# Float64 weights split into two float32r parts: from sums on the tensor engine to a 16-bit addition and subtractions on the vector engine, with a new order of the first steps

## The chip, the cores and the metric

The kernel runs on one core of one Trainium2 chip. The metric is the device time of one execution in microseconds (us); several executions are timed and the median is given.

## The reference

The kernel computes a chunked attention and then a feed-forward layer with a softmax-linear-unit. q, k and v have the shape (8, 8, 576, 64): batch, heads, sequence, head dimension. The attention is local to chunks of 64 positions. The weights `w_in` (512 x 1024) and `w_out` (1024 x 512) arrive as float64; the rest is float32.

```
scores = scale * q_c @ k_c.T          # per chunk of 64, scale = 1/sqrt(64)
attn   = exp(scores - max) / (sum + 1e-9)
x      = (attn @ v_c) as (4608 tokens, 512)
h      = x @ w_in                     # 4608 x 1024
solu   = h * softmax(h)
ln     = (solu - mean) / sqrt(var + 1e-6) * g_ln
out    = ln @ w_out                   # 4608 x 512, float32
```

## The kernel before, in words

The 4608 tokens are 36 tiles of 128. For each tile i the steps are: q and k with the head dimension on the partitions, scores (`scores`), softmax (`softmax_a`, `softmax_e`, `softmax_b`), the transposed attention, the products with v (`values`), the split of x into a high and a low float32r part (`x_high`, `x_low`), the first layer (`ffn_in`, 24 matmuls of 128x512 into the PSUM tile `ph`, which has one buffer), the maximum of h and the exponential (`solu_a`), the product and the mean (`solu_b`), the variance (`variance`), the transposed z and its split, and the second layer (`ffn_out`, 24 matmuls into a PSUM tile `po`, in three thirds of eight). Each float32 product is three float32r products: high by low, high by high and low by high.

The first five tiles and the preparation of the weights are written out by hand in the string `START` (from line 19). A word there is one step; a step that yields is named again for each further part, so `N:0:0` stands twice, first for the transposes on the tensor engine and then for the copy out of PSUM. The order of the words is the order of the instructions in every engine's queue (tensor PE, vector DVE, scalar ACT, GpSimd POOL, and SP, which issues most DMAs); a program behind the kernel places the semaphores, and each engine works its queue strictly in order. From tile 5 on (`for i in range(first, NT)`) a regular loop takes over. Its first large step is `ffn_in(5)`, called M:5 below.

The words that matter here: `P` loads a unit of raw weights (units 0 to 3 are 128 rows each of `w_in`, units 4 to 7 are 256 rows each of `w_out`, 1 MB each; `P0` and `P1` load unit 0 in halves), `n` loads q and k of a tile naturally, `v` loads v, `g` loads the gains, `q` loads q and k in transposable blocks for later tiles. `N` transposes q or k of a tile on PE, `S` is the scores, `A` and `B` the softmax, `T` the transposes of the attention, `V` the values and the split of x, `M` the first layer, `X` and `Y` the two halves of the solu, `R` the variance, `Z` and `z` the turn of z, `F` a third of the second layer and `o` its store.

A unit of weights is prepared like this before the change. Of each float64 the upper 32-bit word, read as a float32, is clamped (`c`, first part: POOL, for unit 4 DVE, 128x1024), rescaled by an activation (`c`, second part: ACT) and shifted left by three bits on DVE (`C`): that is the float64 cut off to float32, the tile `w_a`. ACT rounds it to float32r, times the gain for `w_out` (`t`, the tiles `wi_h`, `wo_h`). DVE masks the exponent (`r`, into `w_p`) and multiplies it with the lower word (into `w_r`): the rest that the cut lost. The low part is then a sum in PSUM (`D`, `unit_rest`, twice a unit): the identity times `w_a`, minus the high part, plus `w_r`; three matmuls written, four executed, because the float32 one runs as two. For `w_out` the identity is a diagonal of gains that POOL makes. The sum in `po` is then copied to `wi_l` or `wo_l`, by ACT, or by DVE for the two pairs in `EV_DVE`.

PSUM before: `ph` two banks, `sx` two banks (scores and values of a tile in START), `tp` two banks (the transposes of START through `bank()`; in the loop the same banks are the second `sx`, named `sy`), `po` two buffers of one bank (sums of `unit_rest` and of the second layer). The tail uses `bank()` as well: the two transposes of the last tile's z, and one half of the last output.

Of the kernel before, what the change touches and what calls it, by code (L numbers as in the profile page):

```python
# [57 lines left out]
def chunk_attention_then_solu_ffn(  # L58
# [10 lines left out]
    nc = tc.nc  # L69

    B, H, S, D = q.shape
    DM, FF = H * D, g_ln.shape[0]
    P = 128
# [10 lines left out]

    EV_DVE = ((1, 0), (5, 1),)
    NV_DVE = ((0, 0), (0, 1), (1, 0), (1, 1), (3, 0), (6, 0), (9, 1),)
# [22 lines left out]

    TP = ps_t.tile([P, 2, FF // 2], F32, name="tp")  # L110
    banks = 0

    def bank():
        nonlocal banks
        banks += 1
        return TP[:, banks % 2]

# [6 lines left out]
    g_sb = const.tile([P, NFC], F32, name="g_sb")  # L124
    ident_r = const.tile([P, P], F32R, name="ident_r")
    nc.vector.tensor_copy(out=ident_r, in_=ident)
    minus_r = const.tile([P, P], F32R, name="minus_r")
    nc.vector.tensor_scalar(
        out=minus_r, in0=ident, scalar1=-1.0, scalar2=None, op0=ALU.mult
    )  # L130


    const.tile([P, 80], F32, name="pad")
    wi_h = const.tile([P, NCC, FF], F32R, name="wi_h")
# [33 lines left out]

    scaled, tops, lows, diags = {}, {}, {}, {}

    def unit_scale(x):

        hi = raws[x][:, :, :, 1]
        y = scaled[x] = work.tile([P, 2, HALF], F32, name="w_a")
# [7 lines left out]
    def unit_top(x):  # L186
# [13 lines left out]
        tops[x] = a, lo  # L200

    def unit_high(x):
        kind, m = UNITS[x]
        a, lo = tops[x]
# [8 lines left out]
        tops[x] = a, lo, top  # L213

    def unit_low(x):
        kind, m = UNITS[x]
        a, lo = tops[x][:2]
        au = a.bitcast(U32)
        r = work.tile([P, 2, HALF], F32R, name="w_r")
        ru = work.tile([P, 2, HALF], U32, name="w_p2", tag="a_b", bufs=1)  # L220
        dve.tensor_scalar(
            out=ru, in0=au, scalar1=0xFF800000, scalar2=None, op0=ALU.bitwise_and
        )
        dve.scalar_tensor_tensor(
            out=r, in0=lo, scalar=2.0 ** -52, in1=ru.bitcast(F32),
            op0=ALU.mult, op1=ALU.mult,
        )
        if kind == "out":
            for y in range(2):
                one = small.tile([P, P], F32, name="g_diag", bufs=2)  # L230
                one_r = small.tile([P, P], F32R, name="g_diag_r", bufs=2)
                for t in (one, one_r):
                    pool.tensor_scalar(
                        out=t, in0=ident, scalar1=g_sb[:, 2 * m + y:2 * m + y + 1],
                        scalar2=0.0, op0=ALU.mult, op1=ALU.add,
                    )
                diags[x, y] = one, one_r
        lows[x] = r

    def unit_rest(x, y):  # L240

        kind, m = UNITS[x]
        (a, _, top), r = tops[x], lows[x]
        if kind == "in":
            one, one_r = ident, ident_r
            d = wi_l[:, m, y * HALF:(y + 1) * HALF]
        else:
            one, one_r = diags.pop((x, y))
            d = wo_l[:, 2 * m + y, :]
# [101 lines left out]

    st = {}


    sx = ps_a.tile([P, 2, 2, HP, CH], F32, name="sx")
    sy = TP.rearrange("p j (s a k) -> p j s a k", s=2, k=CH)

    def attn(i):
        return sy if order.on and i % 2 else sx

    def scores(i):
        sx = attn(i)
        for hp in range(HP):
            for c in range(2):
                for j in range(2):
                    rows, cols = slice(j * D, (j + 1) * D), slice(c * CH, (c + 1) * CH)
                    pe.matmul(
                        sx[cols, j, 0, hp],
                        QT[i][rows, hp, cols],
                        KT[i][rows, hp, cols],  # L370
                        start=True,
                        stop=True,
                    )
# [6 lines left out]
    def softmax_a(i):  # L380
        sv = attn(i)[:, :, 0].rearrange("p j a k -> p a j k")
        nmax = small.tile([P, HP, 2], F32, name="s_nmax")
# [76 lines left out]
    def values(i):  # L459
        sx = attn(i)  # L460
        for hp in range(HP):
            for j in range(2):
                for c in range(2):
                    rows = slice(c * CH, (c + 1) * CH)
                    pe.matmul(
                        sx[j * D:(j + 1) * D, c, 1, hp],
                        V[i][rows, 2 * hp + j, :],
# [17 lines left out]
    def x_high(i):  # L485
        xv = attn(i)[:, :, 1].rearrange("p c a t -> p a c t")
        xh = work.tile([P, NCC, P], F32R, name="x_h")
# [5 lines left out]
    def x_low(i):  # L493
        xv = attn(i)[:, :, 1].rearrange("p c a t -> p a c t")
        xhv, xlv = (x.rearrange("p a (c t) -> p a c t", t=CH) for x in st[i, "x"])
        dve.tensor_tensor(out=xlv, in0=xv, in1=xhv.bitcast(F32), op=ALU.subtract)
# [33 lines left out]
    def solu_b(i):  # L530
# [15 lines left out]
        st[i, "z"] = z, esum  # L546

    def variance(i):
# [17 lines left out]
    def z_turn(i):  # L566
        z, _ = st[i, "n"]
        if i % 2 == 0:
# [30 lines left out]
    def z_transpose(i, f):  # L599

        z, _ = st[i, "n"]
        pt = bank().rearrange("p (a t) -> p a t", t=P)
# [125 lines left out]
    def product():  # L728
# [8 lines left out]
        "T": attn_transpose, "U": attn_turn, "V": start_values, "c": unit_scale,  # L737
        "C": unit_top, "t": unit_high, "r": unit_low, "D": unit_rest, "M": ffn_in, "X": solu_a, "Y": solu_b,
        "R": variance, "Z": z_turn, "z": z_half, "F": product, "o": store,
# [124 lines left out]
```

## Time and profile before

| | |
|---|---|
| median of three timed executions | 502.07 us (503.82, 501.36, 502.07) |
| span of the profiled execution | 501.8 us; no other time of that execution is listed |
| instructions | 11184 |
| tile 5's first layer (M:5) begins | 106.62 us |
| granted TensorE clock, mean over the span | 0.997 |

Times in the views are us from the span's start. A row of the windows gives a stretch, its length, the busy time of PE, PE's weight loads, DVE, ACT and POOL with counts in brackets, the granted clock of PE, the share of the DMA engines and GB/s. A row of the grouped instructions gives line, engine, operation, output<-inputs, shapes and count, then the total busy us, the mean ns of one, and the idle time before them with what ended it. All instructions of the ordered engines carry one line (L49, a helper), so the groups are told apart by tile names. A matmul's modelled duration is longer than the time between two of them, because they overlap: 24 matmuls of 128x512 with 0.39 us each take about 5.45 us in a row.

### The profile page before, as it was taken

What the parts mean: (1) busy time and instruction counts of PE and PEld (TensorE: products, weight loads), DVE (VectorE), ACT (ScalarE), POOL (GpSimd) and SP (SyncE); (2) the same over time, 40 slices, a digit from 0 to 9 for tenths busy, and PEclk for the clock granted to TensorE, in tenths of its full rate; (3) what the DMA queues carried; (4) which work ended last, traced back from release to release, by engine and by line L of the source; (5) the groups of instructions that cost most, each with busy time, mean ns of one, the idle gap of its engine ahead of it and who ended that gap; (6) DMA issues with size and microseconds to landing.
All of it is one profiled execution on the core that took longest, in us unless ns stands there. A gap on an engine that the chain in (4) does not pass through costs nothing.

```text
span 501.8 us, 11184 instructions
## 1 busy us (share of the span) xinstructions
PE 482.5 (96%) x4248; PEld 391.5 (78%) x4248; DVE 376.7 (75%) x529; ACT 261.7 (52%) x434; POOL 146.4 (29%) x305
## 2 busy tenths in 40 slices
PE   2799998999999999999999999999999999999997
PEld 1467676788888888888888888888888888888876
DVE  3697886659795988787878787878887887954430
ACT  2578875445454555545464545545455454544451
POOL 2124340153241325050505051505142323323300
PEclk9999998999999999999999999999999999999999
DMA  9986884594968687869725778767771716153211
GB/s 267 317 180 169 175 151 103 100 216 82 208 121 185 126 182 170 176 158 163 173 58 146 148 176 142 182 112 194 125 189 35 193 34 183 45 145 85 65 62 42
DMA packets 195908, 72.57 MB, mean 145 GB/s; under 512 B 180048, under 2 KB 180560, under 8 KB 195472
## 3 DMA queue, kind: packets, MB, share of 16 engines
q1 hardware_dynamic: 189008, 58.49, 53.6%
q0 software_dynamic: 6272, 12.60, 9.7%
q10 hardware_dynamic: 576, 0.79, 0.5%
q8 instruction: 33, 0.54, 0.5%
q14 instruction: 19, 0.16, 0.1%
HBM read 37.23 MB, written 9.44 MB: 93 GB/s over the span
## 4 chain that ended last, share of the span: by engine, by line
PE 92%; ACT 4%; DVE 1%; issue 1%; DMA 1%; ACTq 0%; SPq 0%
PE po L49 42%; PE ph L49 39%; PE tp L49 7%; PE sx L49 5%; ACT attn_t L49 1%; DMA nat<-in_q_dram 1%; ACT wo_h L49 1%; ACT z L49 0%; ACT z_h L49 0%; ACT o_sb L49 0%; DVE s_e L49 0%; DVE qT L49 0%; DVE h_nmax L49 0%; ACT kT L49 0%; ACT qT L49 0%
## 5 line engine op out<-in xcount | busy, mean ns | idle before, releaser
L49 PE MATMUL ph<-wi_l,x_h 128*128 128x512 f32 x288 | 113.5, 394 | 0.0
L49 PE MATMUL ph<-wi_h,x_h 128*128 128x512 f32 x288 | 112.8, 392 | 0.0
L49 PE MATMUL po<-wo_l,z_h 128*128 128x512 f32 x280 | 111.2, 397 | 0.1
L49 PE MATMUL po<-wo_h,z_l 128*128 128x512 f32 x280 | 109.5, 391 | 0.0
L49 PE MATMUL po<-wo_h,z_h 128*128 128x512 f32 x280 | 109.3, 391 | 0.0
L49 ACT ACTIVATE z<-ph,h_nmax 128x1024 f32<-128x1024 f32 x36 | 40.2, 1116 | 132.1 <-DVE h_nmax L49 132.0
L49 POOL TENSOR_TENSOR u<-ssq,eps 128x1 f32<-128x1 f32 x36 | 7.2, 200 | 247.9 <-ACT sq L49 247.9
L49 PE MATMUL ph<-wi_h,x_l 128*128 128x512 f32 x288 | 78.0, 389 | 0.0
L49 POOL DMA_DIRECT2D z_t<-z_b x136 | 67.7, 505 | 17.0 <-DVE z_b L49 15.2
L49 DVE TENSOR_REDUCE h_nmax<-ph 128x1 f32<-128x1024 f32 x36 | 44.0, 1223 | 36.7 <-PE ph L49 36.7
L49 PEld LDWEIGHTS ph<-wi_l,x_h 128*128 128x128 f32 x288 | 54.6, 190 | 11.7 <-PE po L49 0.4
L49 PEld LDWEIGHTS ph<-wi_h,x_h 128*128 128x128 f32 x288 | 54.6, 190 | 11.3
L49 PEld LDWEIGHTS ph<-wi_h,x_l 128*128 128x128 f32 x288 | 54.1, 188 | 11.4
L49 PEld LDWEIGHTS po<-wo_l,z_h 128*128 128x128 f32 x280 | 52.5, 188 | 11.9 <-ACT z_h L49 0.5
L49 PEld LDWEIGHTS po<-wo_h,z_l 128*128 128x128 f32 x280 | 52.6, 188 | 11.6 <-DVE z_l L49 0.6
L49 PEld LDWEIGHTS po<-wo_h,z_h 128*128 128x128 f32 x280 | 52.6, 188 | 10.5
L49 DVE TENSOR_TENSOR z_l<-z_t,z_h 128x1024 fp32r<-128x1024 f32 (+1 forms) x35 | 40.7, 1163 | 20.4 <-ACT z_h L49 20.4
L49 DVE SCALAR_TENSOR_TENSOR z<-ph,z 128x1024 f32<-128x1024 f32 x36 | 43.9, 1220 | 14.9 <-ACT z L49 14.9
L49 ACT ACTIVATE z<-z,z_sum 128x1024 f32<-128x1024 f32 x32 | 36.9, 1154 | 22.2 <-DVE z L49 21.6
L49 DVE STREAM_TRANSPOSE z_b<-z 128x1024 f32<-128x1024 f32 x33 | 40.0, 1211 | 6.2 <-ACT z L49 3.1
L49 ACT ACTIVATE o_sb<-po,r 128x512 f32<-128x512 f32 (+1 forms) x36 | 24.2, 673 | 31.5 <-POOL r L49 20.3
L49 ACT ACTIVATE sq<-z 128x1024 bf16<-128x1024 f32 x36 | 37.5, 1043 | 0.1
(99 smaller groups left out, 656.4 us busy)
## 6 DMA issues: line engine op xcount, KB each, us to landing
out_dram<-o_sb SPq DMA_DIRECT2D x33, 256.0 KB, 2.5
v_sb<-in_v_dram SPq DMA_DIRECT2D x32, 256.0 KB, 4.3
z_t<-z_b POOLq DMA_DIRECT2D x128, 64.0 KB, 2.7
z_t<-z_b SPq DMA_DIRECT2D x128, 64.0 KB, 2.9
q_st<-in_q_dram SPq DMA_DIRECT2D x96, 72.0 KB, 3.2
k_st<-in_k_dram SPq DMA_DIRECT2D x96, 72.0 KB, 3.1
w_raw<-in_moe_w_out_dram SPq DMA_DIRECT2D x4, 1024.0 KB, 7.4
attn_t<-a_b POOLq DMA_DIRECT2D x60, 64.0 KB, 3.6
```

The costliest lines, as they stand in the source:

```text
L49: ins = make(*args, **kwargs)
```

## The change

- `unit_low` (`r`) and the sums of `unit_rest` on PE are gone, with `ident_r`, `minus_r`, the tiles `w_r`, `w_p`, and the diagonals on POOL.
- `C` becomes `unit_round`: after the shift, a second DVE instruction adds the lower word, times 2^-29, to the lower 16 bits of each float32, as unsigned 16-bit numbers with a step of two. It turns the cut into a rounding to float32, and what is below float32 is dropped.
- `D` becomes a subtraction on DVE, 128x512, in one part: the rounded weight (times the gain for `w_out`) minus its high part. All its operands lie in SBUF.
- `bank()` returns a buffer of `po` in place of half of `tp`, so the transposes of START and of the tail share two buffers with the sums of the second layer. `sy` has its two banks alone; in START the scores of a tile go to `sx` and its values to `sy`.
- `w_a` has four buffers instead of two.
- `START` is written anew. The same words stand in it, apart from `r` (gone), `C` (two parts) and `D` (one part), in another order: q and k of tiles 0 and 1 are loaded ahead of the weights, units 3 and 7 earlier, and the blocks `q` later. The loop from tile 5 is the same.

```diff
 START (before)
-P0 n:0 v:0 P1 P:1 n:1 P:2 v:1 P:3 N:0:0 N:0:1 N:0:0 n:2 N:0:1 g P:4 S:0 c:0 A:0 c:0 A:0 C:0 B:0
-c:1 t:0 c:1 r:0 T:0 T:0 N:1:0 C:1 N:1:1 D:0:1 N:1:0 t:1 r:1 D:0:0 D:0:1 V:0 N:1:1 D:0:0 c:2
-D:1:1 V:0 v:4 n:3 c:2 V:0 D:1:0 D:1:1 C:2 M:0 r:2 t:2 c:3 S:1 D:1:0 c:3 D:2:0 A:1 N:2:0 D:2:0
-N:2:1 C:3 D:2:1 N:2:0 n:4 r:3 N:2:1 P:5 t:3 M:0 v:3 P:6 A:1 c:4 D:3:1 D:2:1 B:1 c:4 D:3:0 D:3:1
-M:0 D:3:0 C:4 r:4 t:4 T:1 M:0 T:1 N:3:1 X:0 V:1 N:3:1 D:4:0 X:0 S:2 D:4:0 Y:0 N:3:0 V:1 N:4:1
...
 START (after)
+n:0 N:0:0 N:0:1 n:1 N:0:0 N:1:0 N:0:1 S:0 N:1:1 P0 N:1:0 P1 A:0 N:1:1 c:0 P:3 P:1 A:0 n:2 P:2
+v:0 c:0 B:0 c:3 C:0 c:1 n:3 S:1 N:2:1 C:0 c:3 t:0 A:1 D:0:0 N:2:0 c:1 C:3 A:1 c:2 N:2:1 C:1 C:3
+T:0 P:7 N:2:0 C:1 n:4 S:2 P:4 N:3:0 B:1 T:0 c:2 t:3 N:3:1 A:2 C:2 A:2 N:3:0 C:2 t:1 v:1 N:3:1
+V:0 P:6 v:2 D:0:1 n:5 S:3 g P:5 V:0 T:1 D:1:1 V:0 T:1 A:3 M:0 N:4:0 N:4:1 c:7 D:1:0 N:4:0 t:2
+B:2 v:5 n:6 D:3:1 A:3 c:4 D:2:0 D:2:1 M:0 T:2 D:3:0 B:3 T:2 V:1 v:7 c:6 M:0 c:5 N:4:1 M:0 c:4
+X:0 N:5:0 V:1 c:6 S:4 V:1 X:0 N:5:0 N:5:1 C:6 V:2 V:2 Y:0 c:7 C:4 v:3 N:5:1 C:6 V:2 T:3 M:1 c:5
+C:4 T:3 N:6:1 N:6:0 A:4 n:7 N:6:1 C:5 X:1 S:5 Y:0 z:0:1 v:4 X:1 t:6 C:7 V:3 N:6:0 z:0:0 Y:1 M:2
+z:0:1 n:8 z:0:0 t:4 V:3 C:5 C:7 z:0:1 z:0:0 A:5 t:5 N:7:0 R:0 A:4 N:7:0 Q:2 N:7:1 D:4:0 S:6 q:8
+D:5:0 N:7:1 N:8:1 N:8:0 D:4:1 X:2 N:8:1 q:8 X:2 B:4 Y:2 V:3 A:6 N:8:0 D:6:0 n:9 Y:1 A:5 F t:7
+Y:2 T:4 D:5:1 T:4 Z:2 B:5 M:3 X:3 R:2 V:4 A:6 S:7 D:7:1 T:5 D:6:1 D:7:0 F F B:6 X:3 T:5 V:4 q:8
+o:0 V:4 Y:3 q:8 Y:3 v:6 z:1:1 V:5 z:1:0 z:1:0 z:1:1 M:4 A:7 Z:3 U:6 z:1:0 R:3 N:9:0 A:7 z:1:1
+N:9:0 F X:4 B:7 R:1 N:9:1 F X:4 U:7 N:9:1 F Y:4 V:5 o:1 Y:4 V:5 R:4

 bank
-        nonlocal banks
-        banks += 1
-        return TP[:, banks % 2]
+        return ps_o.tile([P, FF // 2], F32, name="po")
...
 unit_round (was unit_top), after the shift by three
+        yield
+        half = a.bitcast(U16).rearrange("p x (n two) -> p x n two", two=2)[:, :, :, 0]
+        dve.scalar_tensor_tensor(
+            out=half, in0=lo, scalar=2.0 ** -29, in1=half, op0=ALU.mult, op1=ALU.add
+        )
...
 unit_low: removed
-        dve.tensor_scalar(
-            out=ru, in0=au, scalar1=0xFF800000, scalar2=None, op0=ALU.bitwise_and
-        )
-        dve.scalar_tensor_tensor(
-            out=r, in0=lo, scalar=2.0 ** -52, in1=ru.bitcast(F32),
-            op0=ALU.mult, op1=ALU.mult,
-        )
...
 unit_rest
-        ps = ps_o.tile([P, HALF], F32, name="po")
-        pe.matmul(ps, one, a[:, y], start=True, stop=False)
-        pe.matmul(ps, minus_r, top[:, y], start=False, stop=False)
-        pe.matmul(ps, one_r, r[:, y], start=False, stop=True)
-        yield
-        if (x, y) in EV_DVE:
-            dve.tensor_copy(out=d, in_=ps)
-        else:
-            act.copy(d, ps)
+            dve.tensor_tensor(
+                out=wi_l[:, m, y * HALF:(y + 1) * HALF], in0=a[:, y],
+                in1=top[:, y].bitcast(F32), op=ALU.subtract,
+            )
+        else:
+            dve.scalar_tensor_tensor(
+                out=wo_l[:, 2 * m + y, :], in0=a[:, y],
+                scalar=g_sb[:, 2 * m + y:2 * m + y + 1],
+                in1=top[:, y].bitcast(F32), op0=ALU.mult, op1=ALU.subtract,
+            )
...
 attention tiles
-    sy = TP.rearrange("p j (s a k) -> p j s a k", s=2, k=CH)
+    sy = ps_t.tile([P, 2, 2, HP, CH], F32, name="sy")
-    def attn(i):
-        return sy if order.on and i % 2 else sx
+    def attn(i, part):
+        return (sx, sy)[i % 2 if order.on else part][:, :, part]
```

More of the change, by code (lines that the diff above doesn't have):

```diff
@@ L11 @@
 U32 = mybir.dt.uint32
+U16 = mybir.dt.uint16
 AF = mybir.ActivationFunctionType
@@ L82, in chunk_attention_then_solu_ffn @@
     assert FF == 32 * 32
-    EV_DVE = ((1, 0), (5, 1),)
     NV_DVE = ((0, 0), (0, 1), (1, 0), (1, 1), (3, 0), (6, 0), (9, 1),)
@@ L106, in chunk_attention_then_solu_ffn @@
     )
-    TP = ps_t.tile([P, 2, FF // 2], F32, name="tp")
-    banks = 0
     def bank():
-        nonlocal banks
-        banks += 1
-        return TP[:, banks % 2]
+        return ps_o.tile([P, FF // 2], F32, name="po")
     ident = const.tile([P, P], F32, name="ident")
@@ L124, in chunk_attention_then_solu_ffn @@
     g_sb = const.tile([P, NFC], F32, name="g_sb")
[L125 to L129, printed above, removed]
-    )
-    const.tile([P, 80], F32, name="pad")
+    const.tile([P, 336], F32, name="pad")
     wi_h = const.tile([P, NCC, FF], F32R, name="wi_h")
@@ L167, in load_pair @@
         raws[x] = raw
-    scaled, tops, lows, diags = {}, {}, {}, {}
+    scaled, tops = {}, {}
     def unit_scale(x):
         hi = raws[x][:, :, :, 1]
-        y = scaled[x] = work.tile([P, 2, HALF], F32, name="w_a")
+        y = scaled[x] = work.tile([P, 2, HALF], F32, name="w_a", bufs=4)
         top = 1.875 * 2.0 ** 16
@@ L184, in unit_scale, with unit_round @@
         act.activation(y, y, AF.Prelu, scale=2.0 ** -112, alpha=-(2.0 ** 32))
-    def unit_top(x):
+    def unit_round(x):
         kind, m = UNITS[x]
@@ L199, in unit_top @@
         )
-        tops[x] = a, lo
+        yield
[3 more added lines that the diff above has]
+        )
+        tops[x] = a
     def unit_high(x):
         kind, m = UNITS[x]
-        a, lo = tops[x]
+        a = tops[x]
         if kind == "in":
@@ L212, in unit_high @@
                 act.activation(top[:, y], a[:, y], AF.Copy, scale=g)
[L213 to L220, printed above, removed]
-        dve.tensor_scalar(
-            out=ru, in0=au, scalar1=0xFF800000, scalar2=None, op0=ALU.bitwise_and
-        )
-        dve.scalar_tensor_tensor(
-            out=r, in0=lo, scalar=2.0 ** -52, in1=ru.bitcast(F32),
-            op0=ALU.mult, op1=ALU.mult,
[L227 to L238, printed above, removed]
+        tops[x] = a, top
     def unit_rest(x, y):
         kind, m = UNITS[x]
-        (a, _, top), r = tops[x], lows[x]
+        a, top = tops[x]
         if kind == "in":
-            one, one_r = ident, ident_r
-            d = wi_l[:, m, y * HALF:(y + 1) * HALF]
-        else:
-            one, one_r = diags.pop((x, y))
-            d = wo_l[:, 2 * m + y, :]
-        ps = ps_o.tile([P, HALF], F32, name="po")
-        pe.matmul(ps, one, a[:, y], start=True, stop=False)
-        pe.matmul(ps, minus_r, top[:, y], start=False, stop=False)
-        pe.matmul(ps, one_r, r[:, y], start=False, stop=True)
-        yield
-        if (x, y) in EV_DVE:
-            dve.tensor_copy(out=d, in_=ps)
-        else:
-            act.copy(d, ps)
+            dve.tensor_tensor(
+                out=wi_l[:, m, y * HALF:(y + 1) * HALF], in0=a[:, y],
+                in1=top[:, y].bitcast(F32), op=ALU.subtract,
+            )
+        else:
+            dve.scalar_tensor_tensor(
[3 more added lines that the diff above has]
+            )
     QT, KT, V, QS, KS = {}, {}, {}, {}, {}
@@ L349, in turn_natural @@
             act.copy((QT, KT)[x][i], pt)
-    st = {}
+    st, ZS = {}, {}
     sx = ps_a.tile([P, 2, 2, HP, CH], F32, name="sx")
-    sy = TP.rearrange("p j (s a k) -> p j s a k", s=2, k=CH)
-    def attn(i):
-        return sy if order.on and i % 2 else sx
+    sy = ps_t.tile([P, 2, 2, HP, CH], F32, name="sy")
+    def attn(i, part):
+        return (sx, sy)[i % 2 if order.on else part][:, :, part]
     def scores(i):
-        sx = attn(i)
+        s = attn(i, 0)
         for hp in range(HP):
@@ L367, in scores @@
                     pe.matmul(
-                        sx[cols, j, 0, hp],
+                        s[cols, j, hp],
                         QT[i][rows, hp, cols],
@@ L380, in softmax_a @@
     def softmax_a(i):
-        sv = attn(i)[:, :, 0].rearrange("p j a k -> p a j k")
+        sv = attn(i, 0).rearrange("p j a k -> p a j k")
         nmax = small.tile([P, HP, 2], F32, name="s_nmax")
@@ L459, in values @@
     def values(i):
-        sx = attn(i)
+        s = attn(i, 1)
         for hp in range(HP):
@@ L465, in values @@
                     pe.matmul(
-                        sx[j * D:(j + 1) * D, c, 1, hp],
+                        s[j * D:(j + 1) * D, c, hp],
                         V[i][rows, 2 * hp + j, :],
@@ L485, in x_high @@
     def x_high(i):
-        xv = attn(i)[:, :, 1].rearrange("p c a t -> p a c t")
+        xv = attn(i, 1).rearrange("p c a t -> p a c t")
         xh = work.tile([P, NCC, P], F32R, name="x_h")
@@ L493, in x_low @@
     def x_low(i):
-        xv = attn(i)[:, :, 1].rearrange("p c a t -> p a c t")
+        xv = attn(i, 1).rearrange("p c a t -> p a c t")
         xhv, xlv = (x.rearrange("p a (c t) -> p a c t", t=CH) for x in st[i, "x"])
@@ L546, in solu_b @@
         st[i, "z"] = z, esum
+        ZS[i] = z
     def variance(i):
@@ L566, in z_turn @@
     def z_turn(i):
-        z, _ = st[i, "n"]
+        z = ZS[i]
         if i % 2 == 0:
@@ L599, in z_transpose @@
     def z_transpose(i, f):
-        z, _ = st[i, "n"]
+        z = ZS[i]
         pt = bank().rearrange("p (a t) -> p a t", t=P)
@@ L737, in chunk_attention_then_solu_ffn @@
         "T": attn_transpose, "U": attn_turn, "V": start_values, "c": unit_scale,
-        "C": unit_top, "t": unit_high, "r": unit_low, "D": unit_rest, "M": ffn_in, "X": solu_a, "Y": solu_b,
+        "C": unit_round, "t": unit_high, "D": unit_rest, "M": ffn_in, "X": solu_a, "Y": solu_b,
         "R": variance, "Z": z_turn, "z": z_half, "F": product, "o": store,
```

8 lines of the change are left out of this document (removed).

## The prediction

> **What bounds the kernel now.** I read the page's busy times and its chain first, then the windows, cut where the regular loop begins, then the chain in order of time and the waits.
>
> ```profile
> span 501.8 us, 11184 instructions
> PE 482.5 (96%) x4248; PEld 391.5 (78%) x4248; DVE 376.7 (75%) x529; ACT 261.7 (52%) x434; POOL 146.4 (29%) x305
> ...
> PE 92%; ACT 4%; DVE 1%; issue 1%; DMA 1%; ACTq 0%; SPq 0%
> ```
>
> PE sets the time: 92% of the chain. Where it does so with work that the change touches is a question of the stage:
>
> ```profile
> core 0: us, PE busy (x) PEld busy (x) DVE busy (x) ACT busy (x) POOL busy (x), PEclk, DMA share, GB/s
> 0.00:7.69 7.69, 2.21 (x8) 1.44 (x8) 0.36 (x3) 1.28 (x1) 0.86 (x10) 1.00 0.92 218
> 7.69:39.60 31.91, 24.83 (x176) 16.70 (x176) 24.02 (x35) 19.91 (x31) 8.29 (x8) 1.00 0.99 266
> 39.60:106.62 67.02, 64.16 (x617) 49.23 (x618) 50.27 (x75) 42.67 (x83) 22.43 (x39) 0.97 0.70 144
> 106.62:501.80 395.18, 391.34 (x3449) 324.12 (x3447) 302.02 (x417) 197.88 (x321) 114.85 (x249) 1.00 0.60 133
> ```
>
> The cuts are DVE's first copy out of PSUM (7.69), the first X (39.60) and M:5 (106.62). From M:5 on PE is busy 391.3 of 395.2 us, and there the change moves only the tail. So nearly all that it can bring is an earlier M:5. Before M:5 PE is busy 88.99 of the 98.93 us after 7.69, and DVE 74.29: PE leads, DVE is a close second with 24.6 us of slack. Where DVE's slack lies the waits of DVE before M:5 tell:
>
> ```profile
> DVE qT L49 <- PE tp L49: 9.1, 3, 5.9
> DVE h_nmax L49 <- PE ph L49: 4.5, 4, 2.5
> DVE s_nmax L49 <- PE sx L49: 4.0, 2, 2.8
> ```
>
> The three longest, 17.6 us, are all waits for PE. An edit that takes work off PE lets DVE close up, until DVE's own queue is the limit.
>
> **The change part by part.** *Removed from PE:* sixteen pairs of sums. Their cost is not the modelled duration but the place that they take in the queue, from the chain:
>
> ```profile
> 28.60 1.52 PE po L49 x4
> ...
> 30.98 1.33 PE po L49 x4
> 32.32 1.39 PE ph L49 x6
> 33.71 2.65 PE po L49 x8
> ```
>
> Four matmuls are one half-unit: 1.33 us (two in a row 2.65). 16 x 1.33 = 21.3 us. PE's queue before M:5 falls from 88.99 to about 67.7 us.
>
> *DVE.* These rows price it:
>
> ```profile
> L49 DVE SCALAR_TENSOR_TENSOR w_r<-w_raw,w_p 128x1024 fp32r<-128x1024 uint32 x8 | 10.6, 1330 | 0.3
> L49 DVE TENSOR_SCALAR w_p<-w_a 128x1024 uint32<-128x1024 uint32 x8 | 5.6, 704 | 0.2
> L49 DVE TENSOR_TENSOR z_l<-z_t,z_h 128x512 fp32r<-128x512 f32 x4 | 2.8, 692 | 6.2 <-ACT z_h L49 6.2
> L49 DVE CAST wo_l<-po 128x512 fp32r<-128x512 f32 x1 | 0.7, 681 | 0.0
> L49 DVE CAST wi_l<-po 128x512 fp32r<-128x512 f32 x1 | 0.7, 677 | 0.0
> L49 ACT CAST wi_l<-po 128x512 fp32r<-128x512 f32 x7 | 4.1, 585 | 6.6 <-PE po L49 6.6
> L49 ACT CAST wo_l<-po 128x512 fp32r<-128x512 f32 x7 | 4.0, 588 | 0.6 <-PE po L49 0.6
> ```
>
> Out go eight masks (5.6), eight products (10.6) and two copies (1.4), 17.6 us. In come sixteen subtractions; the same shape with both operands in SBUF takes 0.692, so 11.1 us. And eight 16-bit additions, which no row shows: 128x1024, two operands, both with a step of two. The nearest row is the product that they replace, same shape, same lower word with the same step: 1.33 each, 10.6. The ends: 0.70, the rate of the mask, if 16 bits run faster (5.0 us less in all), and twice 1.33, if a write of half a word costs double (10.6 more). I take 1.33. Net 11.1 + 10.6 - 17.6 = +4.1: DVE's queue becomes 74.3 + 4.1 = 78.4 us. Its last 0.7 (the x_low of tile 5) now stands behind the last Y, and M:5's first sixteen matmuls don't need it, so 77.7 us lie ahead of M:5. The shift stays.
>
> *ACT* loses fourteen copies (8.1 us) and goes from 62.6 to 54.5; *POOL* loses sixteen diagonals. Neither leads, so I count nothing for them.
>
> DVE is now the longest queue: 77.7 against PE's 67.7 and ACT's 54.5. M:5 comes at DVE's first copy plus 77.7 plus DVE's idle time.
>
> *The moved loads.* Ahead of q of tile 0, SP now issues nothing:
>
> ```profile
> 0.72 0.39 SPq L49 DMA_DIRECT2D w_raw<-in_moe_w_in_dram  x1
> 1.17 0.42 SPq L49 DMA_DIRECT2D nat<-in_q_dram  x1
> ...
> 5.42 2.23 PE L49 MATMUL tp<-ident,nat 128*128 128x128 f32 x8 [5.42 <-DMA nat<-in_q_dram]
> ...
> 7.69 0.69 DVE L49 COPY qT<-tp 128x512 f32<-128x512 f32 x1 [5.92 <-PE tp L49]
> ...
> 9.07 1.11 POOL L49 TENSOR_SCALAR w_a<-w_raw 128x1024 f32<-128x1024 f32 x1 [7.64 <-DMA w_raw<-in_moe_w_in_dram]
> 10.21 1.06 ACT L49 ACTIVATE w_a<-w_a 128x1024 f32<-128x1024 f32 x1 [8.21 <-POOL w_a L49]
> ```
>
> q goes out 0.45 us earlier and no longer shares the DMA engines with half a megabyte of weights (at 218 GB/s some 2.4 us of all engines). I put DVE's first copy at 6.0 instead of 7.69; the ends are 5.3 and 7.2. Unit 0 now stands behind two q-k pairs, 2.1 MB instead of 1.8 MB with its second half; at 266 GB/s that is 1 us later, about 10. With the clamp and the activation (1.1 each) its shift comes at about 12.3. By then DVE has done four copies (0.69 each) and the softmax of tile 0 (nmax, sum, two products and a reciprocal, 3.1), 5.9 us: 6.0 + 5.9 = 11.9, so 0.4 idle. Further along, unit 5 is the last needed, 12.3 MB into SP's list: 1.5 + 12.3 / 0.266 = 47.7 us. Its shift stands 40 us into DVE's queue, at about 49 with the idle time so far: just in time. Unit 6's load waits for unit 2's buffer, free at about 27, which SP's place in the list allows. The 32 block loads `q` are moved behind all weights.
>
> *DVE's idle time, from the order of the words and the durations of M and of the exponential:*
>
> ```profile
> 61.26 5.45 PE ph L49 x24
> ...
> 102.54 3.65 PE po L49 x16
> ...
> L49 ACT ACTIVATE z<-ph,h_nmax 128x1024 f32<-128x1024 f32 x36 | 40.2, 1116 | 132.1 <-DVE h_nmax L49 132.0
> ```
>
> Eight matmuls of F are 1.82. 0.4 at unit 0; 1.0 because t:0 stands behind unit 3's activation in ACT's queue and D:0:0 behind t:0; 0.5 at unit 1's shift; 2 at X:0, since D:3:0 is followed on DVE by B:3 alone (1.8 us) while PE still has V:1 and two parts of M:0 (1.39 each) to do. From X:1 to X:3 DVE has 5.9 to 7.3 us of other work queued between a Y, which frees `ph`, and the next X, and M takes 5.45: no wait. Between Y:3 and X:4 only 4.7 are queued: 0.9. Behind M:4, PE has three F and two N left, 6.4 us (a transposed half tile is 0.44 to 0.46 in the chain), DVE 5.4: 1.0 more to M:5. Between an X and its Y stand 1.4 us on DVE against the exponential's 1.12, its read-out of 0.2 and the wait: 0.1 each, 0.5. That is 6.3.
>
> To this come collisions with POOL, which the trace shows:
>
> ```profile
> 26.21 1.58 POOL L49 TENSOR_SCALAR w_a<-w_raw 128x1024 f32<-128x1024 f32 x1 [2.29 <-PE po L49]
> ...
> 26.85 2.02 DVE L49 SCALAR_TENSOR_TENSOR w_r<-w_raw,w_p 128x1024 fp32r<-128x1024 uint32 x1
> ```
>
> Side by side the product took 2.02 instead of 1.23 and the clamp 1.58 instead of 1.11. The sixteen subtractions read two operands from SBUF like this product, where the copies that they replace read PSUM. Of eight products one was hit; 24 such instructions beside the same seven clamps and four means let me put 2 us, between 0 and 8. The Trainium skill (SBUF — State Buffer, Who interferes with whom) says that a vector instruction with two SBUF inputs and a GpSimd instruction that reads SBUF lock each other out for the whole instruction. Fully blocked, a clamp of 1.11 before each of eleven POOL instructions would cost DVE up to 12 us by that rule; the overlap above cost 0.8, less than a whole clamp, so it began in the middle.
>
> Sum: 6.0 + 77.7 + 6.3 + 2 = 92.0 for M:5 instead of 106.62: 14.6 us earlier.
>
> *PSUM.* The transposes share two buffers with F's sums, so one is left from the first F of tile 0 to its store; there T:4 and T:5 follow each other with M:3 between them. Cover: DVE's queue. I count nothing here, and a wait of about 1.5 us (transpose, copy) a time if it is gone. In the tail there is no cover:
>
> ```profile
> 488.83 0.69 DVE L49 TENSOR_TENSOR z_own<-tp,z_own 128x512 fp32r<-128x512 f32 x1 [1.76 <-ACT z_own L49]
> 489.86 0.60 PE L49 MATMUL tp<-ident,z 128*128 128x128 f32 x4
> ...
> 492.27 0.28 PE L49 MATMUL tp<-wo_l,z_own 128*128 128x256 f32 x1
> ...
> 492.49 0.69 ACT L49 ACTIVATE o_sb<-po,r 128x512 f32<-128x512 f32 x1 [1.40 <-PE po L49]
> ```
>
> The second half of the last output begins at 492.27 in `tp`. It now needs the buffer that the store of tile 34 frees at 493.18: +0.9. The last transpose waits for the first one's subtraction, which ended at 489.52, while it started at 489.86: nothing.
>
> Total: 501.8 - 14.6 + 0.9 = 488.1. The span lies 0.3 under the median of the runs (502.07), so I say 488.4.
>
> **The rivals.** *1, slower: PE loses its clock.* PE is now short of work early, and the trace shows what that does:
>
> ```profile
> 80.00:85.00 5.00, 3.27 (x53) 2.65 (x44) 1.55 (x3) 3.32 (x8) 0.00 (x0) 0.84 0.39 108
> 85.00:90.00 5.00, 5.00 (x19) 3.98 (x19) 3.34 (x6) 0.33 (x1) 0.00 (x0) 0.82 0.00 0
> ...
> 84.05 6.82 PE ph L49 x24
> ```
>
> After a stretch with 3.27 busy of 5, the clock fell to 0.82 over the next five, and a first layer took 6.82 instead of 5.45. Before X:0, PE has about 15 us of work in 34, and it may run at half clock there, hidden behind DVE. Behind X:0 (at about 40) it has 46 us of work in DVE's 52: four M (21.8), six F (10.9) and 13 of small matmuls. At half clock throughout, that is 92: M:5 at 132, 528 us. It decides from a mean clock below 46/66.6 = 0.69 between X:0 and M:5. Against it: at nearly 90% busy the clock should come back, as it did at 87. The Trainium skill (TensorE: Matmul & The Clock Gate, What's actually happening) has the array at half rate after an idle window of about 3.4 us and at full rate after a busy one; by that rule each lapse lasts about one window, as here. 5%.
>
> *2, DVE waits more than I count.* Each M could begin cold (1.4 x 5 = 7 us, partly covered), unit 5 or 4 could come late, the two transpose buffers could add 1.5 us several times, POOL could cost up to 8. One or two of these give 4 to 9 us: 492 to 497. For it: the DMA engines are 99% busy up to 39.60, and the 16 transposed tiles share buffers that F shares. 20%.
>
> *3, the 16-bit addition costs double:* +10.6, which nothing covers now that DVE leads: 499. For it only that no row shows it. 5%.
>
> *4, the start is not bound where I think:* the loads set it throughout, so that M:5 hardly moves, or it doesn't do what it says on PE: 500 to 503. Against it: in 39.60 to 106.62 the DMA share is 0.70. 5%.
>
> **How the numbers follow.** The forecast, 484 to 492, has 65%: its lower end is DVE without idle time beyond 2 us, its upper the bounds of the collisions and of the first copy. Beyond 0.5% (2.5 us, about what a measurement of this kernel can tell) faster are the forecast, rival 2 and most of rival 3: 0.89. Rival 4 and the rest of 3 are the same: 0.06. Rival 1 is slower: 0.05. The range is 482 to 497: down to an addition at the mask's rate, up to rival 2.
>
> **What would show it.** Right: no `po` matmul on `w_a`; M:5 at about 92; DVE busy about 78 us before it and over 85% of the time from its first copy; PE's busy share there lower than DVE's; the addition at 1.2 to 1.4 and the subtraction at 0.69; the loop's 395 us unchanged but for 0.9 at the end. Wrong: DVE idle for more than 12 us between its first copy and M:5; waits of DVE for weights' loads; first layers over 6 us; additions over 2 us.

## The result and the profile after

The changed kernel takes 487.79 us (median of four runs, 487.56 to 488.19); the kernel before, run beside it, took 502.94 us (501.36 to 504.03). The ratio is 0.9705, 95% interval 0.9681 to 0.9729. The profiled execution took 487.9 us with a span of 486.1.

The page of the changed kernel: instructions and busy time, then the chain by engine.

```profile
span 486.1 us, 11024 instructions
...
PE 462.8 (95%) x4184; PEld 381.6 (78%) x4184; DVE 378.2 (78%) x533; ACT 254.1 (52%) x420; POOL 139.8 (29%) x289
...
PE 89%; DMA 7%; ACT 1%; issue 1%; SPq 1%; DVE 0%; ACTq 0%
```

PE lost 20 us of work and the span lost 15.7. DVE's work grew by 1.5 us and yet it has 0% of the chain; loads went from 1% to 7%. The windows of the changed kernel show where the time went. The cuts are DVE's first copy, the first X, the start of M:2, and M:5:

```profile
5.38:38.97 33.59, 21.73 (x264) 16.89 (x264) 29.88 (x48) 19.75 (x32) 6.62 (x6) 0.95 1.10 308
38.97:54.70 15.73, 13.35 (x181) 10.88 (x181) 13.07 (x19) 10.19 (x18) 3.49 (x3) 0.89 0.98 211
54.70:90.49 35.79, 35.50 (x289) 28.98 (x290) 33.21 (x51) 24.85 (x50) 12.74 (x23) 1.00 0.85 150
90.49:486.10 395.61, 391.10 (x3449) 324.05 (x3447) 302.05 (x417) 198.05 (x320) 116.07 (x249) 1.00 0.59 133
```

M:5 comes at 90.49 instead of 106.62: 16.1 us earlier. From there on the kernel takes 395.61 instead of 395.18. The three stretches ahead of M:5 have three different faces. Up to X:0, DVE is busy 29.88 of 33.59 us and the DMA engines are full (a share over 1 is a small excess in the counting), while PE has a third of its time free. From M:2 on PE is busy 35.50 of 35.79 us. In between, neither PE nor DVE is full (13.35 and 13.07 of 15.73 us), but the DMA engines still are (0.98). The chain of the changed kernel in order of time (start, length, what) says the same, from the load of q of tile 0 to M:5:

```profile
7.47 10.62 DMA nat<-in_k_dram
...
24.23 6.63 DMA nat<-in_k_dram
30.85 9.83 DMA nat<-in_q_dram
...
44.91 5.97 PE ph L49 x24
...
54.70 5.78 PE ph L49 x24
...
65.84 5.66 PE ph L49 x24
...
78.50 5.58 PE ph L49 x24
84.08 6.41 PE po L49 x32
90.49 5.44 PE ph L49 x24
```

Up to 40.7 it follows the loads of q and k, and then PE. (Ahead of M:2 it also names a load of v, 3.09 us from 51.44. By the timeline M:1's maximum, exponential and product follow each other with hardly a gap in that time, from 50.91 to 54.64, and M:2 waits for the product.) A chain shows only the last of the things that were waited for: how far the next one was behind it doesn't show. That is what the experiments are for. The waits of the changed kernel up to M:5 (in total, times, longest):

```profile
PE po L49 <- DMA nat<-in_k_dram: 8.1, 3, 6.0
PE po L49 <- DMA nat<-in_q_dram: 7.7, 4, 4.3
DVE qT L49 <- PE po L49: 6.2, 2, 5.4
DVE h_nmax L49 <- PE ph L49: 3.6, 3, 1.6
```

Of DVE's 17.6 us of waits for PE in the kernel before, 10.2 are left (6.2, 3.6, and 0.4 for the scores), 5.4 of them the wait for the first transposes. PE now waits for loads instead: 15.8 us for q and k, against 5.4 before.

### The profile page after: what moved, and what is told of

It is laid out like the page before. It is cut to its first block, busy times and chain, and to the rows that moved or that the text cites. A ratio compares the mean times of both kernels' runs of the same rounds, so it can differ in the third digit from the quotient of the medians.

```text
span 486.1 us, 11024 instructions
## 1 busy us (share of the span) xinstructions
PE 462.8 (95%) x4184; PEld 381.6 (78%) x4184; DVE 378.2 (78%) x533; ACT 254.1 (52%) x420; POOL 139.8 (29%) x289
## 4 chain that ended last, share of the span: by engine, by line
PE 89%; DMA 7%; ACT 1%; issue 1%; SPq 1%; DVE 0%; ACTq 0%
PE po L49 42%; PE ph L49 39%; PE sx L49 4%; DMA nat<-in_k_dram 4%; PE sy L49 3%; DMA nat<-in_q_dram 3%; DMA v_sb<-in_v_dram 1%; SPq L49 1%; ACT o_sb L49 0%; ACT z L49 0%; DVE h_nmax L49 0%; ACT z_h L49 0%; ACT kT L49 0%; DVE z L49 0%; ACTq L637 0%
## 5 line engine op out<-in xcount | busy, mean ns | idle before, releaser
L49 PEld LDWEIGHTS po<-wo_l,z_h 128*128 128x128 f32 x280 | 52.6, 188 | 12.3 <-ACT kT L49 0.5
L49 DVE TENSOR_TENSOR z_l<-z_t,z_h 128x1024 fp32r<-128x1024 f32 (+1 forms) x35 | 40.7, 1163 | 21.3 <-ACT z_h L49 21.3
```

What stands on the lines that cost most here:

```text
L49: ins = make(*args, **kwargs)
```

## The experiments

Twelve kernels ran, each beside the kernel before on the same chip. Two theories stood at the start. **DVE leads** (the prediction's sum): M:5 follows DVE's first copy and DVE's queue. **The rival**: the loads of q and k and PE's queue behind them set M:5, and DVE is merely nearly as late.

**The new arithmetic alone, in the old order with the old banks.** `START` is the old string without `r`, with a second `C` ahead of each `t` and one `D` a half unit; `bank()`, `attn` and the tail are the old ones.

> The new rounding and the subtractions on the vector engine, in the order of steps of the kernel before and with its PSUM banks (transposes in tp, scores and values of a tile in sx). The theory: the time comes from taking 21.3 us of sums off PE, but an order laid out for a leading PE leaves DVE waiting, so only part of it arrives: M:5 at 95 to 101 (90.49 in the changed kernel, 106.62 before), time 492 to 498. Rival: the sums were hidden and the new order alone brings the gain: time 500 to 504. Second rival: the order is of no account: 487 to 489.

Measured: 507.66 us (506.68 to 508.25), ratio 1.012 (1.0096 to 1.0144). It is slower than the kernel before, outside all three ranges that were expected. Its windows, cut at DVE's first copy and at M:5:

```profile
7.70:110.10 102.40, 72.42 (x729) 57.14 (x730) 76.74 (x116) 54.64 (x99) 24.28 (x31) 0.92 0.80 177
110.10:504.90 394.80, 391.01 (x3449) 324.17 (x3447) 301.97 (x417) 197.98 (x321) 114.83 (x249) 1.00 0.59 134
```

PE is relieved by 16.6 us (88.99 to 72.42) and M:5 is still 3.5 us later. What PE waits for instead (this kernel, up to M:5):

```profile
PE tp L49 <- ACT attn_t L49: 8.5, 4, 3.5
PE tp L49 <- DVE s_e L49: 5.5, 2, 4.1
PE tp L49 <- DMA nat<-in_q_dram: 5.4, 1, 5.4
PE ph L49 <- DVE wi_l L49: 5.0, 2, 2.9
PE tp L49 <- ACT qT L49: 4.9, 2, 4.1
```

PE now waits in the places that the sums had filled: for the softmax on DVE, for the copies that empty the halves of `tp`, and for `wi_l`, which DVE makes.

**The same with the new banks, still in the old order.** `bank()`, `attn` and the tail are those of the changed kernel.

> The changed kernel (new rounding, subtractions, new PSUM banks) in the order of steps of the kernel before. With the old banks that order took 507.7 us. Theory (the old order, made for PE sums, makes SP, ACT and DVE wait for each other, the block loads q ahead of the weights among them): the banks give back 1 to 6 us, time 501 to 507, so the order is worth 14 to 19 us with the new sums. Rival (the banks make most of it): under 497.

Measured: 502.55 us (501.48 to 503.52), ratio 0.9988 (0.9972 to 1.0005), M:5 at 105.69. The banks take back what the arithmetic lost, and the two together are worth nothing. Put in last, the rest of the change, the order of the words, brings the whole gain: 0.9988 to 0.9705. In this kernel DVE has nearly the same work ahead of M:5 as in the changed one (76.98 us against 76.16) and PE 4.5 us more (75.11 against 70.58), but 97.99 us pass from first copy to M:5 against 85.11.

```profile
7.70:105.69 97.99, 75.11 (x729) 59.09 (x730) 76.98 (x115) 54.79 (x99) 22.98 (x31) 0.95 0.85 187
```

**The old banks in the new order.** As the changed kernel, with `bank()`, `attn` and the tail of before. In the new order, by its words, the transposes `N:9:0` go into a half of `tp` between the copy and the subtraction of `z:1:1`, so that half of the low part of z of tile 1 is another. The subtraction waits there (2.68 us), but M:4 to M:5 takes 12.04 us as against 11.99 in the changed kernel, so that the wait doesn't move M:5.

```diff
-        return ps_o.tile([P, FF // 2], F32, name="po")
+        banks += 1
+        return TP[:, banks % 2]
```

> The changed kernel with the PSUM banks of the kernel before: the transposes of the start in the two halves of tp, scores and values of a tile of the start both in sx, the second half of the last output in tp. The theory (DVE's queue sets the start, the banks are covered): M:5 within 2.5 us of 90.49, the tail 0.8 us shorter, time 487 to 490. Rival (values and scores in one tile make each other wait): M:5 over 94, time over 491.

Measured: 496.04 us (495.93 to 496.74), ratio 0.9893 (0.9872 to 0.9914); X:0 at 42.63 and M:5 at 99.10. The expectation (487 to 490) missed. In this kernel the longest waits of DVE but for the first, and those of PE for DVE and ACT:

```profile
DVE h_nmax L49 <- PE ph L49: 5.1, 1, 5.1
...
PE tp L49 <- ACT kT L49: 3.6, 3, 2.1
PE sx L49 <- DVE kT L49: 3.5, 2, 2.7
...
PE tp L49 <- ACT qT L49: 3.2, 3, 2.0
```

By M:5 the banks are worth 8.6 us in the new order and 4.4 in the old one (by the times 8.3 and 5.1, measured on different chips). With the old banks, the new order stands at 0.9893 against the 1.012 of the old one.

**Which part of the banks.** Scores and values of a tile both in `sx` again, the transposes in `po`.

```diff
-        return (sx, sy)[i % 2 if order.on else part][:, :, part]
+        return (sx, sy)[i % 2 if order.on else 0][:, :, part]
```

> The changed kernel with scores and values of a tile of the start both in sx, as before the change; the transposes stay in po. The run with all old banks took 496 us. If the sharing of sx is what cost 8 us there (scores of the next tile wait until the split of x has read the values): 494 to 497, M:5 at 97 to 100. If the transposes in tp cost it: 487 to 489.

Measured: 488.04 us (486.76 to 488.19), ratio 0.9691 (0.9669 to 0.9714), M:5 at 90.68. The separate bank for the values brings nothing beside the transposes in `po`. What the banks bring comes from the transposes in the two buffers of `po` instead of the two fixed halves of `tp`. Both are two banks taken in turn; why the halves make PE wait longer for ACT's copies, the runs don't show.

**The changed kernel without the 16-bit addition.** The weights are cut to float32 instead of rounded.

```diff
-        dve.scalar_tensor_tensor(
-            out=half, in0=lo, scalar=2.0 ** -29, in1=half, op0=ALU.mult, op1=ALU.add
-        )
```

> The changed kernel without the eight 16-bit additions, so that the weights are cut to float32 and not rounded; 11.5 us less in DVE's queue, all else the same. The theory (DVE's queue leads): M:5 6 to 10 us earlier, at 80 to 84, with PE as the next limit; time 478 to 482. Rival (the loads set the first 40 us, so that only the four additions behind X:0 count): at most 4 us, M:5 at 86 to 90, time 484 to 488. Second rival (PE leads): no change, 487 to 488.

Measured: 487.80 us (486.62 to 488.1), ratio 0.9721 (0.9698 to 0.9745). The windows of this kernel:

```profile
5.30:89.96 84.66, 69.02 (x733) 55.47 (x734) 66.22 (x108) 54.54 (x99) 21.25 (x31) 0.90 0.98 225
```

DVE has 9.9 us less to do ahead of M:5 (66.22 against 76.16), and M:5 comes 0.5 us earlier; the time is that of the expectation's second rival. By the prediction's sum it would have come at about 80. "DVE leads" falls in this form.

**The addition twice.** A second one, which adds nothing (its factor is 2^-70), stands behind each first.

> The changed kernel with each 16-bit addition written twice, the second one adding nothing; 8 x 1.35 = 10.8 us more in DVE's queue. The theory (DVE's queue leads): M:5 9 to 11 us later, at 99 to 102, time 496.5 to 499. Rival (the loads set the first 40 us): 4 to 6 us later, M:5 at 94 to 97, time 492 to 494.

Measured: 497.15 us (496.84 to 498.44), ratio 0.9918 (0.9889 to 0.9947). X:0 at 44.67 and M:5 at 99.88, 9.4 us later, for 12.5 us more of DVE's work ahead of it; DVE has 10% of this kernel's chain:

```profile
5.30:99.88 94.58, 72.22 (x733) 56.95 (x734) 88.67 (x124) 54.44 (x99) 24.44 (x31) 0.87 0.89 201
...
PE 85%; DVE 10%; issue 1%; ACT 1%; DMA 1%; SPq 0%; ACTq 0%
```

More work on DVE costs three quarters of its time, less work brings nothing: DVE stands level with something else. The next kernels look for what. (Of the 9.4 us, 5.7 come up to X:0 and the rest between X:0 and M:3.)

**Fewer loads, first try.** Units 6 and 7 are not loaded but made from the raw words of units 4 and 5 (the weights of units 6 and 7 are others); once with the addition, and once without.

```diff
     def load_pair(x):
+        if x in (6, 7):
+            return
...
-        hi = raws[x][:, :, :, 1]
+        hi = raws[x if x < 6 else x - 2][:, :, :, 1]
```

> The changed kernel without the loads of units 6 and 7, which are made from the raw words of units 4 and 5 instead (so these weights are others): 2 MB less ahead of q and k of tile 5, all instructions of the engines as before. Theory now (three limits lie close together before M:5: DVE's queue and the loads up to tile 0's X, PE behind it): with DVE's queue as long as ever, tile 0's X moves by less than 1 us from 38.97, M:1 loses only its wait of 1.9 us for tile 5's q; M:5 0.5 to 2.5 us earlier, time 485.5 to 487.5. Rival (the loads alone set the first 40 us): M:5 4 us earlier or more, time under 484.

> The changed kernel without the loads of units 6 and 7 (made from units 4 and 5) and without the eight 16-bit additions (weights cut, not rounded). Taking off 11.5 us of DVE's work alone gave 0.5 us. Theory (DVE's queue and the loads together hold tile 0's X): relieved of both, it comes 3 to 6 us earlier, at 33 to 36, PE's 51 us behind it stay, M:5 at 84 to 88, time 481 to 485. Rival (something else holds the first 40 us, PE's low clock or ACT): the same as with fewer loads alone, within 1 us.

Measured: 489.09 us (488.81 to 490.07) and 489.59 us (488.97 to 489.93), ratios 0.9716 and 0.9726; M:5 at 93.05 and 91.97, both later. Both times lie outside what the theory expected. The edit made a wait of its own, here in the chain of the first of the two and in POOL's part of its timeline:

```profile
33.58 5.95 DMA w_raw<-in_moe_w_out_dram
...
45.68 7.77 PE ph L49 x24
...
39.70 3.23 POOL L49 TENSOR_SCALAR w_a<-w_raw 128x1024 f32<-128x1024 f32 x3 [17.34 <-DMA w_raw<-in_moe_w_out_dram]
```

Unit 7's clamp stands early in POOL's queue and now waits for the load of unit 5, which stands late in SP's list; the clamps and activations behind it come late as well. And the loads taken away stood behind those of tiles 2 and 3, so they could not relieve X:0. These two say nothing on the question, although the second came within 1 us of the first, as its rival (PE's low clock or ACT holds X:0) had it.

**Fewer loads, at the right place.** Units 1 and 3, which stand ahead of q and k of tiles 2 and 3 in SP's list, are made from the words of unit 0; once with the addition, and once without.

```diff
     def load_pair(x):
+        if x in (1, 3):
+            return
...
-        hi = raws[x][:, :, :, 1]
+        hi = raws[0 if x in (1, 3) else x][:, :, :, 1]
```

> The changed kernel, but units 1 and 3 are not loaded: both are made from the raw words of unit 0, so the rows of the first layer's weights that belong to units 1 and 3 are others. 2 MB less stand in SP's list ahead of q and k of tiles 2 and 3; every instruction on DVE, ACT, POOL and PE stays. Theory (up to the first X, the loads of tiles 2 and 3 and DVE's queue end at nearly the same time, so neither alone brings anything): DVE's queue still holds X:0, which moves less than 2 us from 38.97, M:5 at 88.5 to 90.5, time 485.5 to 488. Rival (the loads alone set the time up to X:0): X:0 5 to 7 us earlier at 32 to 34, M:5 at 83 to 86, time 481 to 484.

> As the kernel with units 1 and 3 made from unit 0's words, and the 16-bit addition is left out as well, so that all weights are cut instead of rounded. Theory (two limits side by side up to X:0): with both taken away X:0 comes 3 to 6 us earlier than 38.97, at 33 to 36; PE's 51 us from there to M:5 stay, M:5 at 84 to 88, time 481 to 485, which neither the missing addition alone (487.8) nor the missing loads alone reach. Rival (PE's queue with its order sets it already before X:0): X:0 at 38 to 39, time 486.5 to 488, as without the addition alone.

Measured: 484.72 us (483.75 to 485.46), ratio 0.9668 (0.9638 to 0.9699), and 481.37 us (481.1 to 482.82), ratio 0.9609 (0.9583 to 0.9635). Each one's windows, cut at DVE's first copy, X:0, M:2 and M:5; with the addition:

```profile
5.20:38.51 33.31, 23.80 (x266) 19.16 (x267) 30.39 (x48) 19.29 (x33) 8.10 (x6) 1.00 1.10 272
38.51:51.91 13.40, 12.00 (x181) 9.42 (x179) 13.22 (x19) 10.03 (x19) 4.17 (x2) 1.00 1.08 225
51.91:87.67 35.76, 35.47 (x289) 28.99 (x290) 33.18 (x51) 24.85 (x50) 12.71 (x23) 1.00 0.76 136
```

and without it:

```profile
5.20:35.24 30.04, 20.93 (x264) 16.11 (x264) 26.93 (x44) 19.94 (x33) 7.11 (x6) 0.83 1.11 281
35.24:48.49 13.25, 12.15 (x180) 9.68 (x181) 10.48 (x16) 9.41 (x18) 2.24 (x2) 1.00 1.05 239
48.49:84.20 35.71, 35.42 (x289) 28.98 (x290) 31.00 (x49) 24.85 (x50) 11.89 (x23) 1.00 0.81 149
```

The kernel without the addition, with all loads, has between the same points:

```profile
38.56:54.23 15.67, 12.03 (x180) 9.59 (x181) 10.75 (x16) 10.18 (x18) 2.62 (x3) 1.00 0.99 209
```

Together with the changed kernel that makes a table of four:

| X:0 / X:0 to M:2 / M:5, us | all loads | 2 MB fewer ahead of tiles 2 and 3 |
|---|---|---|
| with the addition | 38.97 / 15.73 / 90.49 | 38.51 / 13.40 / 87.67 |
| without | 38.56 / 15.67 / 89.96 | 35.24 / 13.25 / 84.20 |

Either one alone moves X:0 by less than half a microsecond, both together by 3.7. That is what two limits side by side look like, and X:0 came as the theory said. For M:5 the theory said 88.5 to 90.5 with the addition, and 485.5 to 488 for the time, and both came earlier: there the loads hold something by themselves, behind X:0. From X:0 to M:2 the missing addition brings 0.1 us, the missing loads 2.3, both 2.5. Most of it is q of tile 5, whose transposes stand ahead of M:1 in PE's queue. In the changed kernel PE waits there:

```profile
40.82 0.63 PE L49 MATMUL po<-ident,nat 128*128 128x128 f32 x4 [1.89 <-DMA nat<-in_q_dram]
```

With fewer loads that wait is gone (0.39 us are left of it where the addition is missing too).

**The weights first again.** The word `P0` stands ahead of the first `n:0`, as before the change.

> The changed kernel with one word moved: the first half of unit 0's weights is loaded ahead of q and k of tile 0, as before the change. DVE's first copy should come at 7 to 8 us instead of 5.38 by every theory. If DVE's queue from its first copy on sets the time (the prediction's sum), M:5 and the end move by the same 1.5 to 2.5 us: 489.3 to 490.3. If the loads of tiles 2 and 3, whose order in SP's list stays, and PE behind them set it, X:0 moves by less than 0.7 us and the time is 487.3 to 488.5.

Measured: 488.26 us (487.98 to 489.0), ratio 0.9743 (0.9719 to 0.9766). DVE's first copy comes at 6.50 instead of 5.38, X:0 at 39.2 and M:5 at 90.70: of 1.1 us lost at the start 0.2 arrive. The order in which the loads of tiles 2 to 5 follow is the same in both.

**A better version.** The words `P:7` and `c:7` stand behind `P:5` and the `c:5`; and the tail takes a bank of `sy`, which is empty by then.

```diff
-T:0 P:7 N:2:0 C:1 n:4 S:2 P:4 N:3:0 ...
+T:0 N:2:0 C:1 n:4 S:2 P:4 N:3:0 ...
...
-                ps_o.tile([P, DM], F32, name="po") if x == 0 else bank()
+                ps_o.tile([P, DM], F32, name="po") if x == 0
+                else sy[:, 0].rearrange("p s a k -> p (s a k)")
```

> The changed kernel with two edits. Unit 7 of the weights is loaded, clamped and rescaled behind unit 5 instead of ahead of tile 4's loads, which puts 1 MB less ahead of the loads of tile 4; and the second half of the last output is summed in the first bank of sy, which stands empty by then, instead of the second buffer of po. The last matmuls then don't wait for the store of tile 34: 0.8 us less by the wait that the trace shows there. If the load of unit 7 was no part of what holds X:0, the whole is 486.6 to 487.4. If loads ahead of X:0 count, X:0 comes 1 to 3 us earlier and the time is 484 to 486.5. It may also be worse, if unit 7 now comes late for its part of the second layer of tile 0: then M:5 is later than 90.49 and the time 487.5 to 490.

Measured: 484.98 us (484.71 to 485.31), ratio 0.9675 (0.9653 to 0.9698). The intervals of the ratios of this kernel and of the changed one overlap; the two ran on different chips. Against the kernel with the weights first, which ran on the same chip, it is 3.3 us faster, and those intervals don't overlap. The traces, windows of this kernel, show the two gains apart:

```profile
5.33:38.81 33.48, 21.61 (x266) 16.78 (x267) 30.61 (x48) 20.62 (x33) 7.23 (x5) 0.75 1.08 286
38.81:88.89 50.08, 47.64 (x469) 38.32 (x468) 47.18 (x70) 33.99 (x66) 17.19 (x26) 1.00 0.89 188
88.89:483.50 394.61, 390.91 (x3448) 324.06 (x3447) 301.89 (x417) 198.04 (x320) 115.71 (x249) 1.00 0.59 134
```

From M:5 to the end it takes 394.61 instead of 395.61: that is the tail. M:5 comes 1.6 us earlier. The expectation for this time (484 to 486.5) saw X:0 1 to 3 us earlier; X:0 stayed, and the stretch behind it became shorter: q of tile 5 no longer stands behind unit 7's megabyte, and PE's wait of 1.89 us for it is not in this trace.

In the nine kernels with the new order and the new banks whose M:2 is in the trace's chain, M:2 to M:5 takes the same time: 35.71 to 35.80 us, 35.79 in the changed kernel and 35.73 without the addition. With the addition twice the chain comes back to PE only at M:3, and M:3 to M:5 takes 24.71 us against 24.65. That stretch is PE's alone.

## Why the prediction came out, point by point

**The time** (488.4) was met within 1 us, and M:5 (92.0) within 1.5; the reason given for it was half right, and errors in its terms partly cancelled.

*PE's relief: right, a little large.* 67.7 us were foretold ahead of M:5, 70.58 were measured from the first copy on; 1.1 of the difference is work that stood ahead of the first copy before (2.21 us there, now 1.12), and about 1.2 are M:1 to M:4, which took 22.99 us instead of 21.8. The "about 15 us" of PE's work ahead of X:0, in rival 1, don't fit the prediction's own sum: 67.7 less 46 is 21.7, and 21.73 were measured.

*DVE's queue and its new instructions: the prices right, the sum too large.* 77.7 us foretold and 2 for collisions, 76.16 measured with the collisions in it. The net growth put at 4.1 was 1.87 (74.29 to 76.16). The prices are not the reason. Where DVE doesn't wait, an instruction begins a little ahead of the end of the one before it (the sum at 85.26 while the maximum of 84.12 ends at 85.35), so the groups' times add up to some 5 us more than DVE's busy time here and some 3 in the kernel before, which had more waits. The groups of the changed kernel:

```profile
L49 DVE SCALAR_TENSOR_TENSOR w_a<-w_raw,w_a 128x1024 uint16<-128x1024 uint32 x8 | 11.3, 1442 | 0.0
L49 DVE SCALAR_TENSOR_TENSOR wo_l<-w_a,g_sb,wo_h 128x512 fp32r<-128x512 f32 x8 | 5.5, 746 | 0.0
L49 DVE TENSOR_SCALAR w_a<-w_a 128x1024 uint32<-128x1024 uint32 x8 | 5.5, 686 | 0.8 <-ACT w_a L49 0.8
L49 DVE TENSOR_TENSOR wi_l<-w_a,wi_h 128x512 fp32r<-128x512 f32 x8 | 5.4, 708 | 0.0
```

The addition has the price of the product that it replaces: 1.44 us on average with one disturbed, 1.35 for the other seven. Neither the mask's rate nor the double price came true. The subtractions cost 0.708 and 0.746 on average against the 0.692 put down.

*Collisions with POOL: right in kind, 2 us put down, about 0.9 measured* (0.74 on one addition, 0.11 on one subtraction into `wi_l`, which took 0.80 where the median is 0.69). The subtractions into `wo_l` all take 0.742 to 0.749: that is their price and no collision. The largest, in the timeline of the changed kernel:

```profile
13.39 1.21 POOL L49 TENSOR_SCALAR w_a<-w_raw 128x1024 f32<-128x1024 f32 x1 [1.65 <-DMA w_raw<-in_moe_w_in_dram]
13.68 2.09 DVE L49 SCALAR_TENSOR_TENSOR w_a<-w_raw,w_a 128x1024 uint16<-128x1024 uint32 x1
```

The addition began 0.92 us ahead of the clamp's end and took 0.74 longer than its fellows, while the clamp lost at most 0.1. The other way round, a clamp that began at 20.80, while an addition ran until 21.38, took 1.53 instead of 1.12. The Trainium skill (SBUF — State Buffer, Who interferes with whom) has whoever comes first hold the port and the other blocked until it is done. Both cases agree with that nearly: 0.74 of 0.92 us and 0.41 of 0.58 were lost.

*The start: right at the first step, without effect at the last.* The first copy came at 5.38 (6.0 foretold, 5.3 to 7.2 the ends), unit 0's shift at 12.96 (12.3), X:0 at 38.97 (about 40). But the 1.7 us that the sum gave to the moved loads are hardly there: with the weights first again, 1.1 us at the start became 0.2 at M:5.

*"DVE is now the longest queue": this is the step that failed.* It was read from the whole stretch ahead of M:5, 77.7 against 67.7 us, and the parts of that stretch have different limits. Up to X:0 DVE and the loads hold it side by side, and from X:0 to M:2 the loads alone (the table of four). Behind X:0 the prediction had 46 us of PE's work in a stretch of 52 that it counted as DVE's; measured are 48.85 of PE's (13.35 and 35.50) and 46.28 of DVE's (13.07 and 33.21), in 51.52 us. From M:2 on PE leads again and has no gap. Without the addition DVE had 9.9 us less to do and M:5 came 0.5 us earlier, where a leading DVE would have given nearly all of it.

*The sum was met in part by luck.* The first copy came 0.6 us earlier than foretold, DVE's work with the collisions was 3.5 less than the 79.7 put down, and its idle time 2.7 more (8.95 against 6.3): together 1.5 us.

*That a shorter PE queue lets DVE close up* failed without the rest: in the old order with the new banks DVE stayed idle for 21.0 of 97.99 us, in the changed kernel for 8.95 of 85.11. It is the order that lets it close up.

*PSUM counted at nothing: right about the cost, blind to a gain.* The only wait of PE ahead of M:5 that can be one for a shared buffer is 0.3 us (the second layer's `po` for ACT's copy into `kT`). That the two buffers of `po` would be better for the transposes than the halves of `tp`, by 4 to 9 us, was not seen.

*The tail: right in kind.* +0.9 foretold; the wait in the changed kernel is 0.80, though the time from M:5 to the end grew by only 0.43 (395.18 to 395.61):

```profile
476.57 0.38 PE L49 MATMUL po<-wo_l,z_own 128*128 128x256 f32 x1 [0.80 <-ACT o_sb L49]
```

With the bank of `sy` the time from M:5 to the end fell by 1.0.

*The rivals.* 1 (the clock): it dipped, to 0.89 on the mean of 38.97 to 54.70, far from the 0.69 over the whole stretch to M:5 that it needed. 2 (more waits of DVE): in a small part; its idle time was 8.95 us for 6.3 foretold, and not the 4 to 9 more. 3 (the addition twice as dear): no, but its price was right: the kernel with two of them came at 497.15, for a foretold 499. 4 (the loads set the start throughout): as a forecast wrong; as a mechanism half of what holds X:0, and what holds the stretch from there to M:2.

What stays open: the old arithmetic in the new order wasn't tried. So what the order would be worth without the new arithmetic is not known; the runs show only that the arithmetic and the banks without the order are worth nothing. And the old order was fitted to the new words in one way only; how much of the gain another such fit would have brought isn't shown.

## What to carry to other kernels

In this hand-ordered start, work taken off the leading engine brought nothing until the order was written anew; with nearly the same work on DVE, the stretch took 98 us in the old order and 85 in the new one. Cut the stretch at the points where the limit changes before you sum a queue, and ask of the limit found how far behind it the next one stands: taking work away and adding work to the same engine are two different experiments, and only both together tell a lead from a tie. When either of two suspects alone changes nothing, take both away at once.

## What was not expected of the hardware

The write of the lower halves alone, 16 bits with a step of two from a 32-bit source, costs DVE about as much as a full float32 product of the same shape (1.35 against 1.33 us for 128x1024). And a lower clock of PE did not always show in the time. Up to X:0 the granted clock was 0.95 in the changed kernel, 0.75 in the better version and 1.00 with fewer loads, and X:0 came at 38.97, 38.81 and 38.51. Behind X:0, after PE's wait for q of tile 5, the clock was 0.89 in the changed kernel, and the products with v took longer there than in the better version, which has no such wait and a clock of 1.00 up to M:2. In the changed kernel and in the better version:

```profile
42.73 1.13 PE L49 MATMUL sy<-attn_t,v_sb 64*64 64x64 f32 x32
...
40.67 0.69 PE L49 MATMUL sy<-attn_t,v_sb 64*64 64x64 f32 x32 [0.26 <-DVE x_l L49]
```

M:1, next in the queue, took 5.97 us against 5.44 for M:5.
